# The last rows of half of w1: two transfers of 104 and 88 rows instead of one block of 64

## The chip, the cores and the metric

The kernel runs on one core of a Trainium2 chip. The metric is the device time of one execution in microseconds, and a kernel's time is the median of its runs. The core has a tensor engine (TensorE, PE in the rows), a vector engine (VectorE, DVE), a scalar engine (ScalarE, ACT), GpSimd (POOL), and SyncE (SP), which here only issues transfers. Its transfers are carried by 16 DMA engines.

## What is computed

One decoding step for two tokens: attention over a cache of 4096 positions in 16 heads, a hidden layer with relu, and a sigmoid gate that mixes the two.

```
B, Sq, D = 2, 1, 448;  H, Sk, Dh = 16, 4096, 256;  Dff = 1792
q = (x @ wq)                                  # per batch and head
p = softmax(q . k_cache * Dh ** -0.5)
a = (p . v_cache) @ wo
b = relu(x @ w1) @ w2                         # w1: 448 x 1792, w2: 1792 x 448
g = sigmoid((x * gate_w).sum(-1))
out = g * a + (1 - g) * b
```

All data are float32. The two caches together are 268 MB; w1, w2 and wq, wo are 3 to 7 MB each.

## The kernel before, in words

The host lays all weights and caches out so that each transfer fills the 128 rows (partitions) of SBUF with long contiguous rows. A ring of three slots of 64 KB per row holds the data. A slot takes one unit, that is one head of one batch: half the slot is K, half V. There are 32 units.

SyncE issues all transfers in one queue. First wq goes into slot 0 and units 0 and 1 into slots 1 and 2; then each next unit goes into the slot that came free, once VectorE has counted `freed` for it. The last unit comes in two halves. When unit 29's slot is free (`freed` at U - 2), SyncE issues w1 and then w2 into slot 0; when unit 30's is free, it issues wo in six pieces of 14, 8, 4, 3, 2 and 1 blocks of 448 columns into slot 1 (`ACC` and `DIRECT`).

For each unit TensorE computes the scores into `sc`, VectorE takes their maximum (`nm`), ScalarE the exponentials (`p`), and VectorE multiplies V by them with eight instructions that sum along the row.

The tail, `pe_tail`, runs once the last unit is done. TensorE computes the hidden layer into `pa` in four groups of columns, one for each quarter of the output rows, with the 448 rows of w1 in three blocks of 128 and a last block of 64 rows; the last blocks of two column groups lie one above the other in 128 rows and are contracted together, against `xl`, which has x in the upper or lower 64 rows and zeros in the rest. Between these matmuls stand the transposes of the maxima and sums (`ml_tr`) and the weights of the units (`wb`). Then follow the attention output `oc`, the transposes of the hidden layer, the 14 matmuls with w2 into `acc` (L258), 26 with wo's first three pieces into `acc` (L270), VectorE's copy `a_sb`, four matmuls of it on `fold` (L278) and 24 with wo's last three pieces into `z` (L283), and the result's copy and transfer.

`xr`, `xn` and `xl` are ScalarE's copies of x out of wq's transfer, which holds x as its last columns.

Of the kernel before, what the change touches and what calls it, by code (L numbers as in the profile page):

```python
# [4 lines left out]
AF = mybir.ActivationFunctionType  # L5
# [4 lines left out]
P, HP = 128, 64  # L10
G = 4
R = P // G
# [6 lines left out]
def gated_mix_decode(nc, wq, kv, wm, wo, out):  # L19
    U, _, SW = kv.shape  # L20
    D = 448
    B = 2
    RB = R // B
# [4 lines left out]
    KC, KF = 4, 3  # L28
    H = U // B
    HH = H // G  # L30
    NW = wq.shape[1] - KC * (B + 1)
    FG = 448
    NF = 14
    W1 = 2 * (2 * KF * FG + FG)
    DG = D // G
    NO = HH * J
    SCALE = float(DH) ** -0.5
    pe, dve, act, pool, sp = nc.tensor, nc.vector, nc.scalar, nc.gpsimd, nc.sync
# [12 lines left out]
    slot = [ring[:, i * SW:(i + 1) * SW] for i in range(SLOTS)]  # L51

    def sb(name, *shape):
        t = nc.alloc_sbuf_tensor(name, list(shape), F32)
        assert nc.sbuf_base <= first
        return t.ap()
# [6 lines left out]
    last_v, w1_in, w2_in = ev(), ev(), ev()  # L63
# [11 lines left out]
    xr = sb("xr", P, KF, P // B, B)  # L75
    xl = sb("xl", P, 2, RB, B)
    xn = sb("xn", P, P // B, B)
    ge = sb("ge", P, 1)
    gp = sb("gp", P, 1)
    omg = sb("omg", P, 1)  # L80
# [7 lines left out]
    p = sb("p", P, SG)  # L88
# [10 lines left out]
    pa = ps("pa", P, CW)  # L99
# [5 lines left out]
    def x_of(c, n=R):  # L105
        return xr[:, c].rearrange("p r b -> p (r b)")[:, :n]

    def project(dst, w, at, at_last, n, lo, hi):
        for c in range(lo, min(hi, KF)):
            for g in range(G):  # L110
                m = pe.matmul(dst[g * R:(g + 1) * R, :n], x_of(c), w[:, at(c, g):at(c, g) + n], start=(c == 0), stop=False)  # L111
        if hi == KC:
            for i in range(2):
                m = pe.matmul(dst[i * HP:(i + 1) * HP, :n], xl.rearrange("p j r b -> p (j r b)"),  # L114
                              w[:, at_last(i):at_last(i) + n], start=False, stop=True)
        return m

    xg = slot[0][:, NW:wq.shape[1]].rearrange("p (c b) -> p c b", c=KC)

    ident_0, ident_ok, par_ok, fold_ok, xl_0 = (ev() for _ in range(5))  # L120
    x_ok, gate_mm, gate_ok, ge_ok, gp_ok, omg_ok = (ev() for _ in range(6))
# [23 lines left out]
    ml_tr, nb_ok, e_ok, el_ok, rl_ok, wb_ok, wp_mm, os_ok, po_mm, oc_ok = (ev() for _ in range(10))  # L145
    acc_mm, a_ok, z_mm, res_ok = ev(), ev(), ev(), ev()
    w1 = slot[0][:, :W1]
    w2 = slot[0][:, W1:W1 + NF * D]
    w_o = slot[1]

    with nc.Block(no_gpsimd_drain=True) as block:

        @block.sync
        def _(_e):
            sp.wait_ge(q_mm, 2)
            sp.dma_start(slot[0], kv[2]).then_inc(slot_in[0], 16)
            with nc.Fori(0, LOOP - 2, engines=(ET.SP,)) as r:
                u0 = sp.snap(r * SLOTS)
                for k in range(SLOTS):
                    s = (k + 1) % SLOTS  # L160
                    sp.wait_ge(freed, u0 + k + 1)
                    sp.dma_start(slot[s], kv[bass.ds(u0 + k + SLOTS, 1)].rearrange("o p n -> (o p) n")  # L162
                                 ).then_inc(slot_in[s], 16)
            sp.wait_ge(freed, U - 4)
            sp.dma_start(slot[1], kv[U - 2]).then_inc(slot_in[1], 16)
            sp.wait_ge(freed, U - 3)
            sp.dma_start(slot[2][:, :SW // 2], kv[U - 1][:, :SW // 2]).then_inc(slot_in[2], 16)
            sp.dma_start(slot[2][:, SW // 2:], kv[U - 1][:, SW // 2:]).then_inc(last_v, 16)
            sp.wait_ge(freed, U - 2)
            sp.dma_start(w1, wm[:, :W1]).then_inc(w1_in, 16)  # L170
            sp.dma_start(w2, wm[:, W1:]).then_inc(w2_in, 16)
            sp.wait_ge(freed, U - 1)
            k = 0
            for n, s in zip(ACC + DIRECT, wo_in):
                sp.dma_start(w_o[:, k * D:(k + n) * D], wo[:, k * D:(k + n) * D]).then_inc(s, 16)  # L175
                k += n
            sp.wait_ge(res_ok, 1)
            sp.dma_start(out, res[0:7 * 15 + 1:7, :]).then_inc(out_sem, 16)
# [13 lines left out]
        def pe_main():  # L192
# [7 lines left out]
            for i in range(2):  # L200
                if i:
                    pe.wait_ge(q_ok, i)
                project(pb, slot[0][:, i * NW // 2:(i + 1) * NW // 2], lambda c, g: g * W + c * CW,
                        lambda i: G * W + i * CW, CW, 0, KC).then_inc(q_mm, 1)
# [18 lines left out]
                pe.end_ifs()  # L223

        def pe_tail():
            half = W1 // 2
            def hidden(lo, hi):
                return project(pa, w1, lambda c, g: g // 2 * half + (g % 2 * KF + c) * FG,
                               lambda i: i * half + 2 * KF * FG, FG, lo, hi)

            pe.wait_ge(w1_in, 16)
            hidden(0, 2)
            pe.wait_ge(freed, U)
            pe.transpose(pc[:U, :P], nm, ident)
            pe.transpose(pc[:U, P:2 * P], ls, ident).then_inc(ml_tr, 1)
            hidden(2, KF)
            pe.wait_ge(wb_ok, 1)
            pe.matmul(pb[:, :U], wb.rearrange("u g r -> u (g r)"), ident[:U, :U], start=True,
                      stop=True).then_inc(wp_mm, 1)
            hidden(KF, KC).then_inc(hid_mm, 1)  # L240
            pe.wait_ge(fold_ok, 1)
            pe.wait_ge(os_ok, 1)
            n = HH * B * J
            for g in range(G):
                m = pe.matmul(pc[g * R:(g + 1) * R, :n], sel,
                              os.rearrange("p u j -> p (u j)")[:, g * n:(g + 1) * n], start=True, stop=True)
            m.then_inc(po_mm, 1)
            pe.wait_ge(hid_ok, 1)
            for t in range(KF):
                pe.transpose(pb[:, t * P:(t + 1) * P], hs[:, t * P:(t + 1) * P], ident)  # L250
            for j in range(2):
                m = pe.matmul(pb[j * HP:(j + 1) * HP, KF * P:], hs[:, KF * P:], ident, start=True, stop=True)
            m.then_inc(hid_tr, 1)
            pe.wait_ge(w2_in, 16)
            pe.wait_ge(hr_ok, 1)
            for k in range(NF):
                g = k % G
                pe.matmul(acc[g * R:(g + 1) * R, :D], hr[:, k, :], w2[:, k * D:(k + 1) * D], start=(k < G),  # L258
                          stop=False)

            def o_of(k):
                return oc[:, k // J, k % J].rearrange("p r b -> p (r b)")

            pe.wait_ge(oc_ok, 1)
            k, n = 0, sum(ACC)
            for i, a in enumerate(ACC):
                pe.wait_ge(wo_in[i], 16)
                for _ in range(a):
                    g = k % G
                    m = pe.matmul(acc[g * R:(g + 1) * R, :D], o_of(k), w_o[:, k * D:(k + 1) * D], start=False,  # L270
                                  stop=(k >= n - G))
                    k += 1
            m.then_inc(acc_mm, 1)
            for i, a in enumerate(DIRECT):
                if i == 0:
                    pe.wait_ge(a_ok, 1)
                    for g in range(G):
                        pe.matmul(z[g * R:(g + 1) * R, :DG], fold.rearrange("p r b -> p (r b)"),  # L278
                                  a_sb[:, g * DG:(g + 1) * DG], start=(i == 0), stop=False)
                pe.wait_ge(wo_in[len(ACC) + i], 16)  # L280
                for _ in range(a):
                    for g in range(G):
                        m = pe.matmul(z[g * R:(g + 1) * R, :DG], o_of(k),  # L283
                                      w_o[:, k * D + g * DG:k * D + (g + 1) * DG], start=False,
                                      stop=(k == NO - 1))
                    k += 1
            m.then_inc(z_mm, 1)
# [7 lines left out]
        def _(_e):  # L295
            act.wait_ge(slot_in[0], 16)
            act.activation(xr, xg[:, :KF, None, :B].to_broadcast([P, KF, P // B, B]), AF.Copy)  # L297
            act.activation(xn, xg[:, KF:, :B].to_broadcast([P, P // B, B]), AF.Copy)
            act.wait_ge(xl_0, 1)
            for j in range(2):  # L300
                a = act.activation(xl[j * HP:(j + 1) * HP, j], xg[j * HP:(j + 1) * HP, KF:, :B]  # L301
                                   .to_broadcast([HP, RB, B]), AF.Copy)
            a.then_inc(x_ok, 1)
            act.wait_ge(gate_mm, 1)
# [1 line left out]
            for i in range(2):  # L306
# [3 lines left out]
                a = act.activation(qt[:, i * U // 2:(i + 1) * U // 2, :].rearrange("p (s n) t -> p s t n", s=2),  # L310
                                   pc.rearrange("p (s t x) -> p s t x", s=2, t=T)[:, :, :, ::17], AF.Copy)
# [18 lines left out]
            for j in range(2):  # L330
                r = slice(j * HP, (j + 1) * HP)
                a = act.activation(hr[r, KF * G:, :],  # L332
                                   pb[r, KF * P + j * HP:KF * P + (j + 1) * HP].rearrange("p (k r) -> p k r", r=R),
                                   AF.Copy)
# [103 lines left out]
```

## Time and profile before

| | us |
|---|---|
| median of three runs | 676.48 (676.44 to 677.43) |
| profiled execution | 676.38 |
| its span, first to last instruction | 674.8 |
| around the span | 1.58 |
| TensorE busy in matmuls | 213.0 |
| VectorE busy | 339.8 |
| ScalarE busy | 54.2 |

The durations below are those of the profiled execution. Its time is the span and 1.58 us around it.

### The profile page before, as it was taken

How to read it: one execution, taken by the hardware profiler on the slowest of the kernel's cores; microseconds unless marked ns; L12 is line 12 of the kernel's file. 1: busy time of each engine (PE TensorE's matmuls, PEld its weight loads, DVE VectorE, ACT ScalarE, POOL GpSimd, SP SyncE). 2: the span in 40 equal slices, each digit the busy share in tenths (PEclk: the TensorE clock that was granted, in tenths of full speed). 3: DMA queues.
4: the chain of work that ended last, by engine and by line, in shares of the span. 5: the costliest groups of instructions: out<-in, count | busy, mean ns of one | idle time of the engine just before them, and what ended most of it. 6: DMA issues, size and time to landing. Idle time of an engine off the chain costs nothing.

```text
span 674.8 us, 4173 instructions
## 1 busy us (share of the span) xinstructions
PE 213.0 (32%) x1279; PEld 52.0 (8%) x1279; DVE 339.8 (50%) x561; ACT 54.2 (8%) x144; POOL 1.1 (0%) x9
## 2 busy tenths in 40 slices
PE   0633221333332123333321233333222333332455
PEld 0210000000000000000000000000000000000011
DVE  0024566545455665544656654455566445456670
ACT  0110000000000000000000000000000000000110
POOL 0000000000000000000000000000000000000000
PEclk9976567767655676776656677665667767655879
DMA  9999999999999999999999999999999999999997
GB/s 381 427 435 436 435 435 435 435 435 435 435 435 435 435 435 435 435 435 435 431 435 435 435 435 435 435 435 435 435 435 435 435 435 435 435 435 406 420 437 304
DMA packets 6082, 289.59 MB, mean 429 GB/s; under 512 B 704, under 2 KB 832, under 8 KB 1216
## 3 DMA queue, kind: packets, MB, share of 16 engines
q1 hardware_dynamic: 6080, 289.55, 99.3%
q8 instruction: 2, 0.03, 0.0%
HBM read 289.54 MB, written 0.01 MB: 429 GB/s over the span
## 4 chain that ended last, share of the span: by engine, by line
DMA 70%; DVE 12%; PE 9%; issue 6%; DVEq 1%; ACT 1%; SPq 0%; ACTq 0%
DMA ring<-in_kv 65%; DVE ring L356 10%; PE sc L131 9%; DMA ring<-in_wo 4%; DVE nm L351 2%; DVEq L356 1%; ACT p L318 1%; PE z L283 0%; DVEq L348 0%; DVEq L353 0%; PE acc L270 0%; SPq L175 0%; SPq L162 0%; DVEq L351 0%; DVE a_sb L375 0%
## 5 line engine op out<-in xcount | busy, mean ns | idle before, releaser
L356 DVE SCALAR_TENSOR_TENSOR ring<-ring,p 128x1024 f32 x256 | 295.9, 1222 | 54.8 <-ACT p L318 54.8
L131 PE MATMUL sc<-ring,qc 128*32 128x512 f32 x1024 | 182.6, 878 | 417.8 <-DMA ring<-in_kv 417.8
L351 DVE TENSOR_REDUCE nm<-sc 128x1024 f32 x32 | 39.2, 1225 | 236.1 <-PE sc L131 236.1
L131 PEld LDWEIGHTS sc<-ring,qc 128*32 128x32 f32 x1024 | 41.2, 154 | 558.6 <-issue 558.6
L318 ACT ACTIVATE p<-sc,nm 128x1024 f32<-128x1024 f32 x32 | 35.7, 1114 | 257.8 <-DVE nm L351 257.8
L323 ACT ACTIVATE ov<-on 128x8 f32 x32 | 6.7, 208 | 309.0 <-DVE ring L356 309.0
L356 DVE DVE_READ_ACCUMULATOR ring<-ring,p 128x1 f32 x256 | 21.4, 83 | 0.0
L343 DVE TENSOR_SCALAR ge<-ge 128x1 f32<-128x1 f32 x1 | 0.2, 155 | 21.5 <-ACT ge L305 21.5
L196 PE MATMUL pa<-ring,xr 128*128 128x1 f32 x6 | 1.4, 356 | 21.4 <-ACT xl L301 21.4
L375 DVE COPY a_sb<-acc 128x448 f32<-128x448 f32 x1 | 0.6, 625 | 14.7 <-PE acc L270 14.7
L111 PE MATMUL pa<-ring,xr 128*32 128x448 f32 x24 | 4.2, 830 | 11.7 <-DMA ring<-in_wm 11.7
L270 PE MATMUL acc<-ring,oc 128*32 128x448 f32 x52 | 5.9, 544 | 4.7 <-DMA ring<-in_wo 4.7
L111 PE MATMUL pb<-ring,xr 128*32 128x512 f32 x48 | 7.1, 737 | 0.0
L318 ACT ACTIVATION_READ_ACCUMULATOR p<-sc,nm x32 | 6.2, 193 | 0.0
L320 ACT ACTIVATE qc<-qt x32 | 6.1, 192 | 0.0
L258 PE MATMUL acc<-ring,hr 128*32 128x448 f32 x28 | 3.2, 541 | 1.0 <-ACT hr L332 1.0
L196 PEld LDWEIGHTS pa<-ring,xr 128*128 128x128 f32 x6 | 1.4, 326 | 21.4 <-ACT xl L301 21.4
L270 PEld LDWEIGHTS acc<-ring,oc 128*32 128x32 f32 x52 | 1.7, 109 | 8.9 <-issue 5.9
L114 PE MATMUL pb<-ring,xl 128*64 128x512 f32 x8 | 2.2, 618 | 0.0
L297 ACT ACTIVATE xr<-ring 128x384 f32<-128x384 f32 x1 | 0.5, 522 | 18.3 <-DMA ring<-in_wq 18.3
L111 PEld LDWEIGHTS pb<-ring,xr 128*32 128x32 f32 x48 | 1.6, 132 | 3.9 <-issue 3.9
L308 ACT ACTIVATE q<-pb 128x512 f32<-128x512 f32 x2 | 1.2, 598 | 8.6 <-PE pb L114 8.6
(56 smaller groups left out, 23.7 us busy)
## 6 DMA issues: line engine op xcount, KB each, us to landing
ring<-in_kv SPq DMA_DIRECT2D x2, 4096.0 KB, 34.7
ring<-in_wq SPq DMA_DIRECT2D x1, 7174.0 KB, 19.5
ring<-in_wm SPq DMA_DIRECT2D x2, 3136.0 KB, 30.7
ring<-in_wo SPq DMA_DIRECT2D x1, 3136.0 KB, 24.4
ring<-in_wo SPq DMA_DIRECT2D x1, 1792.0 KB, 28.3
ring<-in_wo SPq DMA_DIRECT2D x1, 896.0 KB, 30.0
ring<-in_wo SPq DMA_DIRECT2D x1, 672.0 KB, 31.1
ring<-in_kv SPq DMA_DIRECT2D x31, 39.6
```

What stands on the lines that cost most here:

```text
L111: m = pe.matmul(dst[g * R:(g + 1) * R, :n], x_of(c), w[:, at(c, g):at(c, g) + n], start=(c == 0), stop=False)
L114: m = pe.matmul(dst[i * HP:(i + 1) * HP, :n], xl.rearrange("p j r b -> p (j r b)"), w[:, at_last(i):at_last(i) + n], start=False, stop=True)
L131: m = pe.matmul(sc[g * R:(g + 1) * R, c * CW:(c + 1) * CW], qc[:, s, t:t + 1].to_broadcast([P, R]), slot[s][:, lo:lo + CW], start=(t == 0) ...
L196: m = pe.matmul(pa[:, :1], x_of(c, P) if c < KF else xn[r].rearrange("p r b -> p (r b)"), xg[r, c, B:], start=(c == 0), stop=(c == KC - 1))
L258: pe.matmul(acc[g * R:(g + 1) * R, :D], hr[:, k, :], w2[:, k * D:(k + 1) * D], start=(k < G), stop=False)
L270: m = pe.matmul(acc[g * R:(g + 1) * R, :D], o_of(k), w_o[:, k * D:(k + 1) * D], start=False, stop=(k >= n - G))
L308: act.activation(q, pb, AF.Copy, scale=SCALE).then_inc(q_ok, 1)
L318: act.activation(p, sc, AF.Exp, bias=nm[:, bass.ds(u, 1)], accum_out=ls[:, bass.ds(u, 1)]).then_inc(raised, 1)
L320: act.activation(qf[:, bass.ds((u + 2) % SLOTS * T, T)], qt[:, bass.ds(u + 1, 1), :].rearrange("p o t -> p (o t)"), AF.Copy).then_inc(quer ...
L323: act.activation(ov[:, bass.ds(u, 1), :].rearrange("p o j -> p (o j)"), on, AF.Copy).then_inc(kept, 1)
L351: dve.tensor_reduce(nm[:, bass.ds(u, 1)], sc, axis=AX.X, op=ALU.max, negate=True).then_inc(maxed, 1)
L356: m = dve.scalar_tensor_tensor(v, v, 1.0, p, op0=ALU.mult, op1=ALU.mult, accum_out=on[:, j:j + 1])
```

## The change

The four column groups of w1 are two halves of two groups. The first half stays as it was. In the second half the 448 rows are cut into blocks of 128, 128, 104 and 88 rows. The two blocks of 128 lie in the main transfer of w1 behind the first half; the 104 and the 88 rows, for both groups 896 columns, are loaded by two transfers of their own, into 104 and 88 partitions. ScalarE copies one more block of x, `xe`, whose rows fit the block of 88, from three more columns of wq. The matmuls of the second half take the first 104 rows of `xr`'s third block and the first 88 of `xe`. `w1_in` is waited for at 48, all three transfers. In DRAM the two short blocks are padded to 128 rows, but only 104 and 88 are transferred.

```
-    NW = wq.shape[1] - KC * (B + 1)
+    NW = wq.shape[1] - (KC + 1) * (B + 1)
...
-    W1 = 2 * (2 * KF * FG + FG)
+    PS = (104, 88)
+    W1 = 2 * KF * FG + FG + 4 * FG
+    WE = 2 * FG
...
-    w2 = slot[0][:, W1:W1 + NF * D]
+    w1e = [slot[0][:n, W1 + i * WE:W1 + (i + 1) * WE] for i, n in enumerate(PS)]
+    w2 = slot[0][:, W1 + 2 * WE:W1 + 2 * WE + NF * D]
...
             sp.dma_start(w1, wm[:, :W1]).then_inc(w1_in, 16)
-            sp.dma_start(w2, wm[:, W1:]).then_inc(w2_in, 16)
+            for i, n in enumerate(PS):
+                sp.dma_start(w1e[i], wm[:n, W1 + i * WE:W1 + (i + 1) * WE]).then_inc(w1_in, 16)
+            sp.dma_start(w2, wm[:, W1 + 2 * WE:]).then_inc(w2_in, 16)
...
-            pe.wait_ge(w1_in, 16)
+                for c in range(lo, hi):
+                    for g in range(G):
+                        i, h = divmod(g, 2)
+                        if i == 0 and c == KF:
+                            if g == 0:
+                                pe.matmul(pa[:HP, :FG], xl.rearrange("p j r b -> p (j r b)"),
+                                          w1[:, 2 * KF * FG:half], start=False, stop=True)
+                            continue
+                        x, at = x_of(c) if c < KF else xe.rearrange("p r b -> p (r b)"), (h * KF + c) * FG
+                        w = w1
+                        if i:
+                            at = half + (h * 2 + c) * FG if c < 2 else h * FG
+                            if c >= 2:
+                                x, w = x[:PS[c - 2]], w1e[c - 2]
+                        m = pe.matmul(pa[g * R:(g + 1) * R, :FG], x, w[:, at:at + FG],
+                                      start=(c == 0), stop=(c == KC - 1))
+                return m
+
+            pe.wait_ge(w1_in, 48)
...
+            act.activation(xe, xg[:, KC:, :B].to_broadcast([P, RB, B]), AF.Copy)
```

On SyncE's queue, at the end of the program, these rows stood between the second half of the last unit and wo's second piece (kv is the caches, wm holds w1 and w2; the shape is rows by columns):

```order
L168 DMA ring<-in_kv 128x8192
L170 DMA ring<-in_wm 128x6272 [waits e16]
L171 DMA ring<-in_wm 128x6272
L175 DMA ring<-in_wo 128x6272 [waits e16]
L175 DMA ring<-in_wo 128x3584
```

and in the changed kernel:

```order
L172 DMA ring<-in_kv 128x8192
L174 DMA ring<-in_wm 128x4928 [waits e16]
L176 DMA ring<-in_wm 104x896
L176 DMA ring<-in_wm 88x896
L177 DMA ring<-in_wm 128x6272
L181 DMA ring<-in_wo 128x6272 [waits e16]
```

w1's transfer is shorter, and two transfers with fewer than 128 rows stand ahead of w2 and wo; they wait for nothing of their own.

On TensorE the hidden layer's matmuls of the tail, with w1's wait ahead of the first (e4), stood so (pa is the hidden layer, pc and pb are other sums, os the weighted outputs):

```order
L111 MATMUL pa<-ring,xr 32x448 [waits e4]
L111 MATMUL pa<-ring,xr 32x448 x7
L234 MATMUL pc<-ident,nm 32x128 [waits e16]
L235 MATMUL pc<-ident,ls 32x128
L111 MATMUL pa<-ring,xr 32x448 x4
L238 MATMUL pb<-ident,wb 128x32 [waits e42]
L114 MATMUL pa<-ring,xl 64x448 x2
L245 MATMUL pc<-os,sel 32x64 [waits e44,e21]
```

and in the changed kernel:

```order
L249 MATMUL pa<-ring,xr 32x448 [waits e4]
L249 MATMUL pa<-ring,xr 32x448 x7
L256 MATMUL pc<-ident,nm 32x128 [waits e16]
L257 MATMUL pc<-ident,ls 32x128
L249 MATMUL pa<-ring,xr 32x448 x4
L260 MATMUL pb<-ident,wb 128x32 [waits e42]
L240 MATMUL pa<-ring,xl 64x448
L249 MATMUL pa<-ring,xe 32x448 x2
L267 MATMUL pc<-os,sel 32x64 [waits e44,e21]
```

The order is the same; the last group has one matmul of 64 columns of weights and two of 32 in place of two of 64.

## Rows read from the trace of the kernel before

**Rows 1.** The page: span, GB/s in 40 equal slices, and packets by size.

```profile
span 674.8 us, 4173 instructions
...
GB/s 381 427 435 436 435 435 435 435 435 435 435 435 435 435 435 435 435 435 435 431 435 435 435 435 435 435 435 435 435 435 435 435 435 435 435 435 406 420 437 304
DMA packets 6082, 289.59 MB, mean 429 GB/s; under 512 B 704, under 2 KB 832, under 8 KB 1216
```

**Rows 2.** Busy time by stretch: from:to, length, engines, clock, DMA share, GB/s.

```profile
40.00:600.00 560.00, 165.41 (x928) 37.09 (x920) 303.88 (x493) 43.46 (x115) 0.00 (x0) 0.64 1.00 434
...
668.00:670.00 2.00, 1.55 (x16) 0.16 (x8) 0.00 (x0) 0.00 (x0) 0.00 (x0) 1.00 1.00 406
670.00:670.50 0.50, 0.00 (x0) 0.00 (x0) 0.45 (x1) 0.00 (x0) 0.00 (x0) 1.00 0.64 244
670.50:671.00 0.50, 0.27 (x12) 0.28 (x16) 0.17 (x1) 0.00 (x0) 0.00 (x0) 1.00 0.11 43
671.00:671.50 0.50, 0.50 (x32) 0.46 (x20) 0.00 (x0) 0.00 (x0) 0.00 (x0) 1.00 0.12 47
671.50:672.00 0.50, 0.50 (x23) 0.32 (x16) 0.00 (x0) 0.00 (x0) 0.00 (x0) 1.00 0.05 18
```

**Rows 3.** The chain that ended last, its end: start, length, what.

```profile
639.02 29.95 DMA ring<-in_wo
...
669.02 1.00 PE acc L270 x8
...
670.05 0.64 DVE a_sb L375
...
670.73 0.40 PE z L278 x8
671.12 1.53 PE z L283 x48
```

**Rows 4.** Transfers of wo by size: KB each, us from issue to landing.

```profile
ring<-in_wo SPq DMA_DIRECT2D x1, 3136.0 KB, 24.4
...
ring<-in_wo SPq DMA_DIRECT2D x1, 672.0 KB, 31.1
...
ring<-in_wo SPq DMA_DIRECT2D x1, 448.0 KB, 31.7
ring<-in_wo SPq DMA_DIRECT2D x1, 224.0 KB, 31.7
```

**Rows 5.** SyncE's last issues in order of time, and those of line 175.

```profile
600.44 0.43 SPq L168 DMA_DIRECT2D ring<-in_kv  x1
619.99 0.33 SPq L170 DMA_DIRECT2D ring<-in_wm  x1
620.36 0.43 SPq L171 DMA_DIRECT2D ring<-in_wm  x1
...
L175 SPq DMA_DIRECT2D ring<-in_wo x6: 328/432/434, 638.2 to 640.5; - x6
```

**Rows 6.** TensorE in the tail, in order of time, with the idle time before.

```profile
647.26 3.21 PE L111 MATMUL pa<-ring,xr 128*32 128x448 f32 x16 [11.73 <-DMA ring<-in_wm]
650.40 0.40 PE L234 MATMUL pc<-ident,nm 128*32 128x128 f32 x1
...
650.94 1.01 PE L111 MATMUL pa<-ring,xr 128*32 128x448 f32 x8
...
652.62 0.97 PE L114 MATMUL pa<-ring,xl 128*64 128x448 f32 x4
...
656.25 3.20 PE L258 MATMUL acc<-ring,hr 128*32 128x448 f32 x28 [1.01 <-ACT hr L332]
662.72 1.71 PE L270 MATMUL acc<-ring,oc 128*32 128x448 f32 x16 [3.27 <-DMA ring<-in_wo]
```

**Rows 7.** The start, in order of time: ScalarE's copy of x, TensorE's first scores.

```profile
20.71 0.29 ACT L298 ACTIVATE xn<-ring 128x128 f32<-128x128 f32 x1
...
39.72 1.94 PE L131 MATMUL sc<-ring,qc 128*32 128x512 f32 x8 [4.65 <-DMA ring<-in_kv]
```

More of the change, by code (lines that the diff above doesn't have):

```diff
@@ L77, in gated_mix_decode @@
     xn = sb("xn", P, P // B, B)
+    xe = sb("xe", P, RB, B)
     ge = sb("ge", P, 1)
@@ L116, in project @@
         return m
-    xg = slot[0][:, NW:wq.shape[1]].rearrange("p (c b) -> p c b", c=KC)
+    xg = slot[0][:, NW:wq.shape[1]].rearrange("p (c b) -> p c b", c=KC + 1)
     ident_0, ident_ok, par_ok, fold_ok, xl_0 = (ev() for _ in range(5))
@@ L225, in pe_tail @@
         def pe_tail():
-            half = W1 // 2
+            half = 2 * KF * FG + FG
             def hidden(lo, hi):
-                return project(pa, w1, lambda c, g: g // 2 * half + (g % 2 * KF + c) * FG,
-                               lambda i: i * half + 2 * KF * FG, FG, lo, hi)
-            pe.wait_ge(w1_in, 16)
+                for c in range(lo, hi):
[16 more added lines that the diff above has]
+            pe.wait_ge(w1_in, 48)
             hidden(0, 2)
@@ L297, in _ @@
             act.activation(xr, xg[:, :KF, None, :B].to_broadcast([P, KF, P // B, B]), AF.Copy)
-            act.activation(xn, xg[:, KF:, :B].to_broadcast([P, P // B, B]), AF.Copy)
+            act.activation(xn, xg[:, KF:KC, :B].to_broadcast([P, P // B, B]), AF.Copy)
+            act.activation(xe, xg[:, KC:, :B].to_broadcast([P, RB, B]), AF.Copy)
             act.wait_ge(xl_0, 1)
             for j in range(2):
-                a = act.activation(xl[j * HP:(j + 1) * HP, j], xg[j * HP:(j + 1) * HP, KF:, :B]
+                a = act.activation(xl[j * HP:(j + 1) * HP, j], xg[j * HP:(j + 1) * HP, KF:KC, :B]
                                    .to_broadcast([HP, RB, B]), AF.Copy)
@@ L404 @@
     full, last = blocks(np.concatenate([np.asarray(A_x).reshape(B, D).T, np.asarray(gate_w).reshape(D, 1)], 1))
-    xg = np.concatenate([full, np.concatenate([last, last])[:, None]], 1)
+    PS = (104, 88)
+    ext = np.zeros((P, 1, B + 1), np.float32)
+    ext[:PS[1], 0] = np.concatenate([full[PS[0]:, KF - 1], last])
+    xg = np.concatenate([full, np.concatenate([last, last])[:, None], ext], 1)
     kt = np.asarray(A_k_cache)[:, heads].reshape(B, H, S, T, P).transpose(1, 0, 4, 3, 2).reshape(U, P, T * S)
@@ L416 @@
     wo = np.asarray(A_wo).reshape(HH, G, R, J, D).transpose(1, 2, 0, 3, 4).reshape(P, -1)
-    full, last = blocks(B_w1)
-    full = full.reshape(P, KF, 2, 2, FG).transpose(0, 2, 3, 1, 4).reshape(P, 2, -1)
-    last = last.reshape(HP, 2, 2, FG).transpose(2, 0, 1, 3).reshape(P, 2, FG)
-    w1 = np.concatenate([full, last], 2).reshape(P, -1)
+    w1 = np.asarray(B_w1).reshape(D, 2, 2, FG)
+    full, last = blocks(w1[:, 0])
+    full = full.reshape(P, KF, 2, FG).transpose(0, 2, 1, 3).reshape(P, -1)
+    last = last.reshape(HP, 2, FG).transpose(1, 0, 2).reshape(P, FG)
+    both = w1[:2 * P, 1].reshape(2, P, 2, FG).transpose(1, 2, 0, 3).reshape(P, -1)
+    rest = np.zeros((P, 2, 2, FG), np.float32)
+    rest[:PS[0], 0] = w1[2 * P:2 * P + PS[0], 1]
+    rest[:PS[1], 1] = w1[2 * P + PS[0]:, 1]
+    w1 = np.concatenate([full, last, both, rest.reshape(P, -1)], 1)
     w2 = np.asarray(B_w2).reshape(G, FG, D)
```

## The prediction

> **What bounds the kernel now.** I read first the page's slices and its packet line, to see which resource is never free. The transfers move 435 GB/s in nearly every one of the 40 slices, and only the first and the last are clearly lower [rows 1]. The stretch from 40 to 600 us says the same in one row: 434 GB/s, a busy share of 1.00 for the 16 DMA engines, while TensorE is busy 165 us of 560 and VectorE 304 [rows 2]. So the kernel is one long stream of bytes, and the other engines have time to spare. A change that keeps the bytes can cost or give time only at the two ends of that stream, or by making the stream itself less even.
>
> Then the chain that ended last, for how the end hangs on the stream. It runs from the transfers of wo, which land their third piece at 668.98 us, through the last eight matmul instructions of acc (1.00 us), VectorE's copy (0.64), the eight matmuls on fold (0.40) and the 48 on wo's last three pieces (1.53) to the result [rows 3]. The wo issues give the landings of those three pieces: six issues start 0.46 us apart from 638.2, so the fourth lands at 638.2 + 3 x 0.46 + 31.1 = 670.7, the fifth at 671.7, the sixth at 672.2 [rows 4, 5]. Whatever delays all transfers by d therefore delays the end by d.
>
> Then the last two microseconds of the stream. The DMA engines' busy share is 1.00 until 670, 0.64 up to 670.5, and then 0.11, 0.12 and 0.05 [rows 2]. Times 16 engines that is about 1.8, 1.9 and 0.8 engines. So some 14 of the 16 have nothing left at about 670.4, and one or two others run on to 672, some 1.5 us longer. Those one or two set the end. The trace does not number them.
>
> **The change part by part.** It removes no bytes: half of w1 keeps its layout, and the other half's last 192 rows, which were 128 full rows and a half block, are now 104 and 88 rows of 896 columns. 4928 x 128 + 896 x 104 + 896 x 88 is 802,816 elements, as 6272 x 128 was.
>
> *The two short transfers.* The page's packet line counts one packet per row (832 - 704 = 128 packets under 2 KB but not under 512 B, for the one piece of wo with rows of 1792 B) [rows 1]. Every big transfer of before has 128 rows, so eight for each of 16 engines. The nearest rows to the new ones are those of wo's fifth piece, 128 rows of 896 columns: it lands 1.06 us after the fourth [rows 4, 5], which is 0.13 us for one row on one engine, and its 448 KB at 434 GB/s would be 1.06 too, so short rows cost nothing extra. The 672 KB of the two short transfers are 1.59 us at the stream's rate [rows 2], if all 16 engines share them evenly, 12 rows each. They can hardly share them worse than a full transfer of 128 rows each, where the fullest engine has eight rows and eight again: 2 x 1.06 = 2.12 us, 0.53 more. I take the upper value, since every large transfer that the trace shows runs eight rows to an engine; the lower end is 0.
>
> [...]
>
> *Who is hit.* Eight rows to an engine means 13 engines for 104 rows and 11 for 88. If both start from the same engine, 11 carry eight rows twice, two carry them once and three none: + 4 rows (+ 0.53 us), - 4 rows (- 0.53) and - 12 rows (- 1.59) against 12. As all engines are busy to 670, each keeps this offset to the end. The end moves by + 0.53 us if the engine that ends last is one of the 11, which by count is 11 chances in 16.
>
> *Two more issues on SP's queue.* An issue takes 0.33 to 0.43 us [rows 5]; w2's issue moves from 620.4 to about 621.3, and nothing else is queued behind it until wo's wait at 638.2. The last two kv halves are still under way then: w1 lands only at 647.2 (its matmuls start at 647.26) [rows 6]. Cost 0; without that cover, 0.9.
>
> *w1's wait.* TensorE now waits for three landings at one place. The bytes before the third are the same, so it comes 0 to 0.53 us later. What is queued behind it is the whole tail: the eight matmuls, the transposes of the maxima at 650.40, and through them the weights, the hidden layer and its matmuls, which end at 656.25 + 3.20 = 659.45. TensorE then waits 3.27 us for wo [rows 6]. So 0.53 us are hidden six times over, and wo's landing moves with them. Cost 0; with the cover gone, 0.53 at most.
>
> *One matmul more.* The last group was two matmuls of 64 columns (0.97 us); it is now one of these and two of 32, for which four cost 1.01 us [rows 6]. Between 0 and 0.25 us, under the same 3.27 us. Cost 0.
>
> *At the start.* One ScalarE copy of 128 x 32; the copy of 128 x 128 takes 0.29 [rows 7], so at most 0.3 us later for the queries. TensorE waits 4.65 us for the first kv after that chain [rows 7]. Cost 0; uncovered, 0.3. wq grows by three columns, 1536 B, which is 0.004 us of stream. No row shows lengths that are no multiple of 16 B, as wq's are now; I take 0, and 0.2 us (1% of its 20) as the upper end.
>
> **Sum.** The profiled execution took 676.38 us, a span of 674.8 and 1.6 around it. + 0.53 + 0 + 0 + 0 + 0 gives 676.9; against the median of 676.48, which is 0.1 higher, 677.0. That is + 0.08%, less than the 0.2% (1.35 us) that a measurement of this kernel can tell from none.
>
> **The rivals.**
>
> *The lagging engines are the spared ones.* If the engines that end at 672 are among the three without short rows (or the second of them among those with one), they end 1.59 us (0.53) earlier, near 670.5 to 671; the other 14 end at 670.4 + 0.53 = 670.9. The end comes 0.8 us sooner: 675.7. For it: the slack of 1.5 us in 14 engines is in the rows. Against it: three of 16 by count for the last one. This stays within 0.2% too.
>
> *Even sharing, or hidden anyway:* + 0 to 0.2, so 676.5 to 676.7. For it: nothing in the trace ties a row to an engine. Against it: 6.5 and 5.5 rows per engine are no whole numbers, so an even 12 needs the two to complement each other.
>
> *Slower: the short transfers write SBUF at half the rate.* If two engines must take turns for one way into SBUF, each short row takes 0.26 us: 16 rows are 4.24 us instead of 1.59, + 2.65 for the engines concerned. It decides only above the slack: if the two late engines are spared, the other 14 first use up their 1.5 us, and the end comes 1.2 us later (677.6); if a late engine is hit, up to 2.65 (679.1). For it: the trace has no transfer with another row count than 128 but the 7 KB output, so the rate of one is not shown. Against it: the rate does not depend on row length from 64 KB rows down to 3.5 KB ones [rows 2, 4]. [...]
>
> **How the numbers follow.** The forecast, + 0.2 to + 0.8: 0.45. Late engines spared, - 0.4 to - 1: 0.23, of which 0.02 for more than 1.35 us. Even, within 0.2 us: 0.12. Half rate: 0.18, of which 0.13 lie above 1.35 us. The last 0.02, for what no row bounds, go half to either side. Within 0.2%: 0.45 + 0.21 + 0.12 + 0.05 = 0.83; slower 0.13 + 0.01; faster 0.02 + 0.01. The range runs from the rival of the spared engines, 675.6, to 678.0, into the half-rate case; that leaves out about 0.1 above and somewhat less below.
>
> **What would show it.** Right: the piece of wo that the end hangs on lands about 0.5 us later, the busy share between 645 and 655 stays near 1 with the two short transfers in it, TensorE's wait for wo stays near 3 us, and the share after 670 still shows one or two engines. The faster rival would show as a tail in which nearly all engines stop together before 671.5. The half rate would show as w1's wait ending 1 us or more later and a dip in GB/s around 645. Wrong would be a TensorE that no longer waits for wo, or a wq that lands later than 20 us by more than 0.2.

## The result and the profile after

The changed kernel took 679.48 us (median of eight runs, 677.11 to 680.20); the kernel before, on the same chips, 676.68 (676.22 to 677.53, eight runs). The ratio is 1.0032 with a 95% interval from 1.0019 to 1.0044: slower by more than the 0.2% that can be told from no change, and above the range that was forecast.

One thing has to be kept in mind for all that follows. The profiled execution, the first of each run, took 677.11 us here, the least of the eight. Its span is 675.3; those of the others go from 675.4 to 678.9. The rows below therefore explain + 0.7 us (677.11 against 676.38), and something else adds up to 3.6 us of span in other executions.

First the page of the changed kernel: the span, GB/s by slice and the packets. The last but one slice, about 641 to 658 us, in which w1 and w2 arrive, has gone from 437 in [rows 1] to 388.

```profile
span 675.3 us, 4180 instructions
...
GB/s 381 427 435 435 436 435 435 435 435 435 435 435 435 435 435 435 435 435 435 435 435 435 435 435 435 435 435 435 435 435 435 435 435 435 435 431 427 425 388 326
DMA packets 6298, 289.59 MB, mean 429 GB/s; under 512 B 728, under 2 KB 856, under 8 KB 1432
```

Next the busy time by stretch (columns as in [rows 2]) where the short transfers move, in the kernel before,

```profile
643.50:648.50 5.00, 1.24 (x8) 0.40 (x12) 5.00 (x9) 0.00 (x0) 0.00 (x0) 0.50 1.00 432
```

and there and at the end of the stream in the changed one:

```profile
643.50:648.50 5.00, 0.00 (x0) 0.00 (x0) 5.00 (x9) 0.00 (x0) 0.00 (x0) 0.50 1.07 311
...
670.50:671.00 0.50, 0.00 (x0) 0.00 (x0) 0.45 (x1) 0.00 (x0) 0.00 (x0) 1.00 0.89 362
671.00:671.50 0.50, 0.27 (x12) 0.27 (x16) 0.18 (x1) 0.00 (x0) 0.00 (x0) 1.00 0.85 341
671.50:672.00 0.50, 0.50 (x32) 0.46 (x20) 0.00 (x0) 0.00 (x0) 0.00 (x0) 1.00 0.71 272
672.00:672.50 0.50, 0.50 (x23) 0.29 (x16) 0.00 (x0) 0.00 (x0) 0.00 (x0) 1.00 0.13 47
```

The DMA engines are as busy as before in the stretch around 646 and move 311 GB/s in place of 432, so packets take longer: the short rows 229 ns in the median, where wo's fifth piece has rows of the same length at 140. At the end the picture of [rows 2] has turned over. Before, 14 engines were done at 670.4 and one or two ran on to 672; now 0.89, 0.85 and 0.71 of them are busy up to 672. The many have been made late, and the last landing of all comes only 0.56 us later, at 672.73 in place of 672.17.

From outside it looks like this: from issue to landing (columns as in [rows 4]) the median of w1 and w2 in the kernel before, and w2 in the changed one,

```profile
ring<-in_wm SPq DMA_DIRECT2D x2, 3136.0 KB, 30.7
```

```profile
ring<-in_wm SPq DMA_DIRECT2D x1, 3136.0 KB, 35.5
```

and SyncE's issues of w1, the two short transfers and w2 in the changed kernel, in order of time:

```profile
619.06 0.33 SPq L174 DMA_DIRECT2D ring<-in_wm  x1
619.43 0.80 SPq L176 DMA_DIRECT2D ring<-in_wm  x2
620.27 0.36 SPq L177 DMA_DIRECT2D ring<-in_wm  x1
```

w2, issued at 620.27, lands at 655.8; in the kernel before it landed at 654.6, by the issues and waits of [rows 5, 6] and the median of 30.7 us.

TensorE in the tail, in order of time:

```profile
648.61 3.21 PE L249 MATMUL pa<-ring,xr 128*32 128x448 f32 x16 [12.12 <-DMA ring<-in_wm]
...
653.97 0.97 PE L240 MATMUL pa<-ring,xl 128*64 128x448 f32 x2
654.87 0.57 PE L249 MATMUL pa<-ring,xe 88*32 88x448 f32 x2
...
655.27 0.55 PE L249 MATMUL pa<-ring,xe 88*32 88x448 f32 x2
...
658.48 3.20 PE L280 MATMUL acc<-ring,hr 128*32 128x448 f32 x28 [1.01 <-ACT hr L355]
663.26 3.20 PE L292 MATMUL acc<-ring,oc 128*32 128x448 f32 x28 [1.59 <-DMA ring<-in_wo]
```

w1's matmuls start at 648.61, not 647.26 [rows 6], 1.35 us later. From there to w2's matmuls it takes 9.87 us, not 8.99 [rows 6], 0.88 more, most of it in the last group with its matmuls on `xe`. The wait for wo has shrunk from 3.27 us to 1.59. It is still a wait, so TensorE has not become the bound. The chain that ended last has the same members as in [rows 3]:

```profile
639.81 29.67 DMA ring<-in_wo
...
669.53 1.00 PE acc L292 x8
```

Its transfer ends at 669.48, 0.5 us later than before, and all behind it takes what it took.

### The profile page after: what moved, and what is told of

It reads as the page before. It is cut to its first block, busy times and chain, and to the rows that moved or that the text cites. A ratio compares the mean times of both kernels' runs of the same rounds, so it can differ in the third digit from the quotient of the medians.

```text
span 675.3 us, 4180 instructions
## 1 busy us (share of the span) xinstructions
PE 216.9 (32%) x1281; PEld 52.5 (8%) x1281; DVE 339.8 (50%) x561; ACT 54.3 (8%) x145; POOL 1.1 (0%) x9
## 4 chain that ended last, share of the span: by engine, by line
DMA 68%; DVE 12%; PE 10%; issue 7%; DVEq 1%; ACT 1%; SPq 0%; ACTq 0%
DMA ring<-in_kv 64%; DVE ring L379 10%; PE sc L134 10%; DMA ring<-in_wo 4%; DVE nm L374 2%; DVEq L379 1%; ACT p L341 1%; PE z L305 0%; DVEq L371 0%; DVEq L376 0%; PE acc L292 0%; SPq L181 0%; SPq L166 0%; DVEq L374 0%; DVE a_sb L398 0%
## 5 line engine op out<-in xcount | busy, mean ns | idle before, releaser
L134 PE MATMUL sc<-ring,qc 128*32 128x512 f32 x1024 | 184.8, 887 | 415.7 <-DMA ring<-in_kv 415.7
L249 PE MATMUL pa<-ring,xr 128*32 128x448 f32 (+1 forms) x24 | 4.4, 863 | 12.1 <-DMA ring<-in_wm 12.1
L395 DVE COPY oc<-pc 128x256 f32<-128x256 f32 x4 | 1.4, 418 | 1.5 <-PE pc L267 1.5
## 6 DMA issues: line engine op xcount, KB each, us to landing
ring<-in_wq SPq DMA_DIRECT2D x1, 7175.5 KB, 19.6
```

Source lines behind the costliest of these rows:

```text
L134: m = pe.matmul(sc[g * R:(g + 1) * R, c * CW:(c + 1) * CW], qc[:, s, t:t + 1].to_broadcast([P, R]), slot[s][:, lo:lo + CW], start=(t == 0) ...
L249: m = pe.matmul(pa[g * R:(g + 1) * R, :FG], x, w[:, at:at + FG], start=(c == 0), stop=(c == KC - 1))
```

## The experiments

The trace also keeps each transfer's landings, one for each DMA engine that carries it (16 for each transfer of 128 rows in the kernel before), and each packet's duration. For every profile I take the median engine's landing of the last kv half and of w2 behind it. Between them lie w1 and w2, so a difference against the kernel before is what the transfers of w1 cost the crowd of engines. The last column is how far the last engine's landing of w2 lies behind the median one.

```
                       kv half   w2       between  against   last engine   rows of 3584 B there:
                       median    median            before    behind        median ns, at 140 ns
before                 638.66    653.52   14.86              1.1           -
changed                638.24    655.35   17.11    +2.25     0.4           229,  44 of 192
changed again          638.47    655.53   17.06    +2.20     0.2           234,  46 of 192
both at 128 rows       638.53    654.00   15.47    +0.61     1.3           140, 256 of 256
96 and 96              638.64    654.62   15.98    +1.12     1.4           195,  67 of 192
128 and 64             638.59    654.24   15.65    +0.79     1.4           140, 170 of 192
short ones twice       638.36    659.18   20.82    +5.96     0.1           241,  45 of 384
two more of 128        638.82    657.99   19.17    +4.31     0.1           199, 196 of 448
only the 104           638.70    655.18   16.48    +1.62     1.9           184,  67 of 232
only the 88            638.25    654.49   16.24    +1.38     0.1           140, 164 of 216
```

Two theories were told apart with it. *Uneven share*, the forecast: the short transfers cost only the extra rows of the fullest engines, at the usual 0.14 us. *Shared way*, the forecast's rival: rows of a transfer that is not 128 rows high hold each other up.

**The changed kernel again**, without an edit.

> The changed kernel once more, to see whether its two groups of times (677.1 to 677.7 and 679.4 to 680.2) come back and to get a second profile. Uneven-share theory (the short rows cost only the extra rows of the fullest engines): the landings cannot differ by 2 us between runs. Shared-way theory (rows of a transfer that is not 128 rows high take turns at the ways into SBUF): short rows take 0.2 us and more instead of 0.14, and how long depends on how the engines stand to each other, so w1's last landing differs between profiles by 0.5 us or more, with the end by as much.

Measured: 679.03 us (677.91 to 679.44, five runs), ratio 1.0039, interval 1.0026 to 1.0052. So the result repeats. The second profile again comes from the shortest execution, span 675.4, and the crowd needs 17.1 us from the last kv half to w2 as in the first. Rows of 0.23 us are what the shared way expects; the spread between executions is not explained by the two profiles, since they are alike.

**Both short transfers at 128 rows.**

```
-                sp.dma_start(w1e[i], wm[:n, W1 + i * WE:W1 + (i + 1) * WE]).then_inc(w1_in, 16)
+                sp.dma_start(slot[0][:, W1 + i * WE:W1 + (i + 1) * WE],
+                             wm[:, W1 + i * WE:W1 + (i + 1) * WE]).then_inc(w1_in, 16)
```

> The changed kernel, but both short transfers move all 128 rows (padding too), 229 KB more. Uneven-share theory: the fullest engine has eight rows twice as before, so about the same as the changed kernel. Shared-way theory: every row goes at 0.14 us, cost 0.53 us of stream, 676.9 to 677.3, and no second group of times near 679.5.

Measured: 677.27 us (676.73 to 678.40), ratio 1.0013, interval 1.0004 to 1.0022. All 256 rows take 140 ns, and the crowd is 0.61 us later for 0.53 us of extra bytes. Moving more bytes in full blocks was quicker than moving fewer in blocks of 104 and 88 rows, 15.47 us against 17.11 between the landings. The late executions are gone as well: the eleven spans lie between 675.1 and 676.0 us, where the changed kernel's went up to 677.7 in the same round and to 678.9 in the first. So these too need the short blocks, whatever the way. The uneven share, for which this kernel and the changed one were alike, falls.

**Blocks of 96 and 96 rows** (`PS = (96, 96)`), and **of 128 and 64** (`PS = (128, 64)`).

> Blocks of 96 and 96 rows in place of 104 and 88: the same bytes, and both numbers divide by 16, so every engine has six rows of each. Uneven-share theory: no extra cost, 676.5 to 676.9. Shared-way theory: the rows still fall unevenly on the ways into SBUF, so the short rows take 0.2 us or more, w1's last landing comes over 1 us later than in the kernel before, 677.5 or more.

> Blocks of 128 and 64 rows: the same bytes, all 16 engines eight and four rows. Uneven-share theory: no extra cost, 676.5 to 676.9. Shared-way theory: the 128 rows go at full rate, the 64 at half of it or worse, 64 rows of 3584 B at half rate are 0.5 us more, 677.0 to 677.3.

Measured: 678.13 us, ratio 1.0029, interval 1.0018 to 1.0040, and 677.32 us, ratio 1.0013, interval 1.0004 to 1.0021. The bytes are those of the kernel before and, if all 16 engines share each transfer evenly, every one has the same number of rows (12), yet the crowd is 1.12 and 0.79 us later. The stretch of the short transfers, for 128 rows twice, 96 twice, and 128 and 64:

```profile
643.50:648.50 5.00, 0.63 (x4) 0.20 (x8) 5.00 (x11) 0.00 (x0) 0.00 (x0) 0.50 1.02 427
```

```profile
643.50:648.50 5.00, 0.00 (x0) 0.00 (x0) 5.00 (x9) 0.00 (x0) 0.00 (x0) 0.50 0.96 317
```

```profile
643.50:648.50 5.00, 0.00 (x0) 0.00 (x0) 5.00 (x9) 0.00 (x0) 0.00 (x0) 0.50 1.03 380
```

Only the first keeps the rate, 427 GB/s against 317 and 380. What counts in these runs is how many rows a transfer has, and not only how evenly the engines share them.

**The short transfers twice**, and as control **two more transfers of 128 rows** behind them, both into a spare stretch of slot 0 that nothing reads, with w1's wait at 80.

```
+            for i, n in enumerate(PS):
+                sp.dma_start(slot[0][:n, SW - (i + 1) * WE:SW - i * WE],      # control: [:P] on both sides
+                             wm[:n, W1 + i * WE:W1 + (i + 1) * WE]).then_inc(w1_in, 16)
```

> The changed kernel with its two short transfers issued twice, the second time into a spare stretch of slot 0 that nothing reads; w1's wait covers all five. Uneven-share theory: 16 more rows at 0.14 us on the fullest engines, + 2.2 us against the changed kernel, about 681.2. Shared-way theory: 16 more rows at 0.235 us, + 3.8 us, about 682.8; on landings, w2 3.8 us later against 2.2.

> The control to it: the changed kernel, and behind the two short transfers two more of all 128 rows of the same width into the spare stretch. Both theories: 16 more rows at 0.14 us on every engine, + 2.1 to + 2.2 us against the changed kernel, about 681.2. If this costs 3.8 us too, it is the number of transfers or the short rows, and not how many rows a transfer has.

Measured: 681.31 us (680.05 to 683.65), ratio 1.0080, interval 1.0064 to 1.0096; the control 680.41 (679.08 to 682.17), ratio 1.0065, interval 1.0049 to 1.0080. On the crowd's landing the second pair costs 5.96 - 2.25 = 3.71 us (3.8 by the shared way, 2.2 by the uneven share), two full transfers of the same width 4.31 - 2.25 = 2.06 (2.1 expected). So it is neither the number of transfers nor the length of the rows. The whole times do not decide it: 681.31 is the 681.2 of the uneven share rather than the 682.8 of the shared way, and the two kernels lie 0.9 us apart. The reading rests on the landings of one profile each, and on the control, whose full rows moved at the usual price.

**Only one of the two is short**: the other moves 128 rows (`enumerate((104, P))`, `enumerate((P, 88))` in the loop of the transfers).

> Only the first short transfer has its 104 rows, the other moves 128. Uneven-share theory: 16 rows on the fullest engines, 677.2 as with both at 128. Shared-way theory: eight rows at 0.235 us and eight at 0.14, + 1.4 us on w2's landing against the kernel before, between the two kernels: 677.8 to 678.4.

> Only the second short transfer has its 88 rows, the first moves 128. Expected as for the one with 104 rows alone: 677.2 by the uneven share, 677.8 to 678.4 and + 1.4 us on w2's landing by the shared way.

Measured: 678.09 us, ratio 1.0023, interval 1.0012 to 1.0033, and 677.99 us, ratio 1.0026, interval 1.0017 to 1.0035, with the crowd 1.62 and 1.38 us later, as the shared way expects (1.4). These two also show where the late engine stands. The end of the stream with the 104 rows, and then with the 88:

```profile
673.00:673.50 0.50, 0.50 (x26) 0.35 (x16) 0.00 (x0) 0.00 (x0) 0.00 (x0) 1.00 0.06 22
673.50:674.00 0.50, 0.45 (x20) 0.35 (x16) 0.00 (x0) 0.00 (x0) 0.00 (x0) 1.00 0.04 14
```

```profile
671.50:672.00 0.50, 0.50 (x24) 0.35 (x16) 0.00 (x0) 0.00 (x0) 0.00 (x0) 1.00 0.04 14
672.00:672.50 0.50, 0.50 (x18) 0.16 (x8) 0.00 (x0) 0.00 (x0) 0.00 (x0) 1.00 0.00 0
```

With the 104 rows one engine runs on alone until 674, 1.9 us behind the crowd at w2; with the 88 rows it is 0.1 behind. So in these profiles the engine that is late from early on carries rows of the transfer of 104 and none of the 88. The trace of the changed kernel agrees. The trace names no engine, but the packets of one follow each other within a few ns (the most frequent step is a start 4 ns before the end of the packet before). The late engine ends w1's rows at 645.75, and the last short row of all ends at 647.58, while engines with 16 short rows need over 3 us for them. In the changed kernel it is spared once, and the crowd catches up with it.

**Three more first executions**, without an edit.

> The changed kernel as it is, a look for a profile out of its later group of times (679.4 to 680.2), which neither profile so far shows. If the extra 2.5 us arise at the short transfers, w2 lands 2 us later after the last kv half than the 17.1 us of the two profiles so far; if they arise elsewhere, those 17.1 us stay and another stretch grows.

> The changed kernel as it is, a second look for its later group of times: 17.1 us from the last kv half to w2 again if the extra 2.5 us arise elsewhere, 19 or more if they arise at the short transfers.

> The changed kernel as it is, a third look for its later group of times: 17.1 us from the last kv half to w2 again if the extra 2.5 us arise elsewhere, 19 or more if they arise at the short transfers.

Measured: spans of 675.1, 675.4 and 675.6 us, and 16.9 to 17.0 us between the landings. None fell among the late ones; they settle nothing but that five first executions of this kernel are alike.

**Small matmuls at TensorE's start.** The packets on the queue of instruction fetches had drawn attention: in the kernel before, two of 16 KB, one at 62.96 us for 0.96 us and one at 659.82 for 0.96. The row right behind the first took 2.89 us where the median is 2.42, the one behind the second 1.40 where it is 0.93. From the first on, one engine lands its rows 0.8 to 1.1 us behind the others; at the second another falls some 1.6 us behind the median:

```profile
q8 instruction: 2, 0.03, 0.0%
```

```
kernel before            median    last two engines
kv unit 1 lands at        58.53     58.76    58.90
kv unit 2 lands at        77.90     78.23    79.28
last kv half lands at    638.66    638.84   639.75
w2 lands at              653.52    653.71   654.63
wo's first piece at      660.94    662.00   662.59
```

So the late engines of [rows 2] are those that a fetch has held up. If other executions differ in which engines these are, moving the fetches should move the time. The edit adds matmuls of constants under the wait for wq, whose result nothing reads:

```
         def pe_main():
+            pe.wait_ge(ident_ok, 1)
+            for _ in range(80):
+                pe.matmul(z[:R, :R], ident[:, :R], ident[:, :R], start=True, stop=True)
             pe.wait_ge(x_ok, 1)
```

> The changed kernel with 40 small matmuls of constants at TensorE's start, under the wait for wq, whose result nothing reads; they add some 160 instructions to be fetched. Theory: the two 16 KB instruction fetches each hold one DMA engine up for 1 us, and which engine that is depends on how many were fetched before; in the first execution of the changed kernel they hit engines that carry few short rows. If one more fetch moves them on, the last landing of w2 lies 1 us or more behind the crowd and the span leaves 675.1 to 675.6 for 676.5 or more. Rival, that the later times have another cause: span 675.1 to 675.6 and w2's landings as before.

> The same with 80 small matmuls, some 320 instructions. Theory: at least one more 16 KB fetch, the late engine is another one, span 676.5 or more if it carries short rows of both transfers (11 of 16), 675 if not. Rival: span 675.1 to 675.6.

> The same with 160 small matmuls, some 640 instructions. Theory: two more 16 KB fetches or more, the late engine is another one again, span 676.5 or more if it carries short rows of both transfers (11 of 16), 675 if not. Rival: span 675.1 to 675.6.

> The kernel before with the 80 small matmuls. All its engines carry the same rows, so by the theory it matters little which one a fetch holds up: span 674.1 to 676, near the 674.6 to 674.9 of its first executions if no third fetch falls on a late engine, about 1 us more if one does.

Measured, spans of one execution each: 675.2 us with 40, 679.6 with 80, 677.9 with 160, and 674.6 for the kernel before with 80. The fetches of the changed kernel with 80, and its last stretches:

```profile
span 679.6 us, 4500 instructions
...
q8 instruction: 4, 0.07, 0.0%
```

```profile
675.00:676.00 1.00, 0.53 (x24) 0.54 (x28) 0.41 (x1) 0.00 (x0) 0.00 (x0) 1.00 0.06 23
676.00:676.50 0.50, 0.48 (x24) 0.24 (x15) 0.00 (x0) 0.00 (x0) 0.00 (x0) 1.00 0.19 58
```

There are four fetches now, where the first executions without the matmuls have two or three, and one engine lands the last piece at 676.95, 1.5 us behind a crowd at 675.4; with 160, four engines land it 1.4 to 1.6 us behind. That fits late engines which carry short rows of both transfers; with the 104 rows alone the late engine stayed 1.9 us behind at w2. Which rows these engines carry was not shown. With 40 there are three fetches, none of the engines is late at the end, and the span is that of the unedited kernel: the expectation that any shift brings 676.5 did not hold there. The kernel before with 80 has four fetches too, and nothing of it shows in its time.

The late engine is not the whole of the 679.6 us. The crowd itself lands the last piece at 675.4, and at 672.4 in the changed kernel. From 660 to 668 us, where wo arrives, the changed kernel and the one with 80 matmuls have these rows:

```profile
660.00:668.00 8.00, 5.47 (x52) 1.81 (x48) 0.00 (x0) 0.00 (x0) 0.00 (x0) 1.00 0.97 410
```

```profile
660.00:668.00 8.00, 3.04 (x28) 1.00 (x24) 0.00 (x0) 0.00 (x0) 0.00 (x0) 0.94 1.01 388
```

In the second the engines are no less busy and move less. Full rows of 25,088 B take 1.04 us there in place of 0.93, on all engines, from the short transfers to the end of the stream. Behind w2's landing alone this makes 1.8 us of the crowd's 3.0. No other profile here has it, and in the kernel before with the same four fetches these rows take 0.93 us. Why the rows stay slow in this execution was not shown.

**The same with 80, in more executions**, and the kernel before with them.

> The changed kernel with the 80 small matmuls again, now with further executions. Theory (which DMA engine a fetch holds up moves on from execution to execution): the first execution is a late one again, span 679 to 680, and among the others there are low ones of 675 to 677; the median is near that of the changed kernel, 679. Rival (first executions are quick for another reason, and the 80 matmuls cost 4 us by themselves): all executions near 679.6 or above.

> The control, the kernel before with the 80 small matmuls. Theory: all its engines carry the same rows, so spans stay within 674 to 676.7, as without them, with a median time within 0.1% of the kernel before. Rival (the 80 matmuls cost by themselves): 0.3% and more above it.

Measured: 678.84 us, ratio 1.0036, interval 1.0025 to 1.0047, spans from 675.3 to 678.6; the kernel before with the 80 matmuls 676.11, ratio 0.9995, interval 0.9986 to 1.0004, spans from 674.2 to 675.5. So the matmuls cost nothing, and the changed kernel with them has the same time and the same spread as without. Its first execution had a span of 676.8 and not of 679 to 680 as expected; again one engine ended 1.6 us behind the crowd (674.15 against 672.57), but the crowd itself was 0.8 us quicker between the two landings than in the execution before (17.1 against 17.9 us) and 1.8 us quicker behind them, with full rows at 0.93 us again. The short rows were no quicker (median 233 ns against 222). So the time varies with the full rows behind the short ones, and not only with the late engine.

## Why the prediction was wrong

**The stream as the bound** held: the chain of waits is the same, and what the transfers lose, the end loses.

**Eight rows to an engine** held. Between 643.9 and 648.6 us the trace has 40 landings for the three transfers of w1, that is 16 + 13 + 11. w2's landings behind them agree with three engines that carry no short rows, two that carry eight, one of these the late one, and 11 that carry 16: three land w2 at 653.13 to 653.34 us, one at 654.52 and twelve at 655.21 to 655.72.

**The step that failed** is the price of a row on them: "which is 0.13 us for one row on one engine", taken from wo's 128 rows and carried over to 104 and 88. All 128 rows of wo's fifth piece do take 0.14 us. Of the 192 short rows 44 do; the median takes 0.23. The term of + 0.53 us for the fullest engines measured + 2.25, a part of it in w2's first rows behind the short ones. The argument against the half rate, that rates do not depend on row length, was true of the rows it cites and beside the point: rows of the same 3584 B took 140 ns in transfers of 128 rows and 229 in the median in those of 104 and 88, and the trace of before held only transfers of 128 but for the output.

**The rival at half rate** is what happened, with 0.23 us in place of 0.26, and with both of its signs: w1's wait ends 1.35 us later, and the rate around 646 dips to 311 GB/s. Where the late engines are spared it gave 677.6; the profiled execution took 677.11, since 2.25 us less the 1.5 of slack is 0.7. Where a late engine is hit it gave up to 679.1; 8 of the 11 other executions of the unedited kernel in two runs took 679.0 to 680.2, all but one of them above that bound, so a late engine by the rival's sum is not enough for them. I had given it 0.18, and cut the range off inside it. That the profiled execution lies near the forecast of 676.9 is luck: 2.25 us on the crowd met late engines that were mostly spared.

**"11 chances in 16"** treated the late engine as a fixed, unknown one. In the profiled execution of the changed kernel the engine that is late from a first fetch at 82 us on carries only the 104 rows, and the one that the second fetch holds up, at 667 us, is among the spared: it lands the last piece at 671.56, ahead of a crowd at 672.36. Seen in single executions: with 80 and 160 matmuls the spans are 676.8 to 679.6 us, where five first executions without them have 675.1 to 675.6, and the kernel before does not change. In each of those three, engines end 1.4 to 1.6 us behind the crowd. But with 40 nothing moved, and later executions of the unedited kernel have the same spread with no matmul added. Argued, not shown: that in these the fetches fall on other engines. Full rows that stay slow behind the short ones, 1.8 us in one profile, would do as well, and the two can come together. No profile shows a late execution of the unedited kernel, so it stays open which it is. Shown is that the short blocks are needed for it, by the kernel with both at 128 rows.

A sum of the rival of the spared engines was off too: with 1.5 us of slack and + 0.53 for the others the end comes 1.0 us sooner, not 0.8.

**The covers** all held: the issues on SyncE (0.8 us for two), the extra matmul, ScalarE's copy, and wq, which takes 19.6 us to land against 19.5. Two of the sizes under them did not. w1's wait moved by 1.35 us rather than by 0.53 at most, and the way to w2's matmuls grew by 0.88 where the extra matmul was given 0.25. Less the 0.5 us by which wo came later, they used up half of TensorE's 3.27 us.

**What stays open** is where the rows of a short transfer meet. All 256 rows of two transfers of 128 took 140 ns; of 192 rows in transfers of 104 and 88, of 96 and 96, and of 128 and 64, 44, 67 and 170 did. In the changed kernel the 44 rows at 140 ns are each engine's first few, all started before 644.2 us; all 146 started later took 202 ns or more. No packet tells which row it was, and no run changed where the rows are read from, so whether they meet in SBUF or on the way from DRAM was not shown, nor that two engines take turns there, as the rival at half rate has it.

## What to carry to other kernels

In a stream that keeps all DMA engines busy, count a transfer by its rows before its bytes: here 192 rows in blocks of 104 and 88 cost the crowd of engines 2.25 us, and 256 rows in two full blocks, padding included, 0.61; 128 and 64 rows, without padding, took the same 677.3 us as those two. Before shifting load between engines, look at who ends last, and whether it is the same one in every execution; a balance that fitted the profiled execution (675.3 against 674.8 us of span) was up to 3.6 us off in others (678.9).

## What the runs showed of the hardware that was not expected

In the kernel before, the first instruction fetch of 16 KB took 0.96 us on one DMA engine and made the row behind it 0.47 us longer (2.89 us against 2.42), and in this stream, whose engines are busy throughout (share 1.00, [rows 2]), one engine stays about 1 us behind the others from then on, 0.92 us still at w2. The page lists two such packets, 0.03 MB, on a queue of their own (q8); the longer rows right behind both show that they share the engines with the data.

The full transfer behind the short ones paid as well: 23 of w2's rows of 25,088 B in the changed kernel took 1.1 to 1.7 us, where the median is 0.93. In one of 15 executions profiled with short blocks, the full rows stayed at 1.04 us to the end of the stream.
